# Loading two batches' values with a cast in the DMA, more zero matmuls early on, and later spreads, in a fused attention and feed-forward kernel

## The chip, the cores and the metric

One core of a Trainium2 chip. The metric is the device time of one execution in microseconds (us). Most executions of one kernel lie within about 1% of each other. Each is put down as fast or slow: for a program on one core, slow means over 1.5% above the fastest execution of the same kernel. Verdicts use fast runs alone, with a 95% interval. Profiles are single executions, and so one profile shows one of the states that a kernel can be in. That matters more than usual here.

## The reference, cut to what matters

```python
# q, k, v: (8 batches, 8 heads, 576 tokens, 64)   window 32, dilation 4
mask_plain = (rel >= 0) & (rel < window)                       # heads 0 to 3
mask_dil   = (rel >= 0) & (rel < 4 * window) & (rel % 4 == 0)  # heads 4 to 7
attn = softmax(where(mask, q @ k.T / 8, -1e9)) @ v             # per batch and head
x = attn.transpose(0, 2, 1, 3).reshape(4608, 512)
h = x @ w_in                                                   # 512 -> 2048
out = (h * sigmoid(beta * h)) @ w_out                          # 2048 -> 512
```

The feed-forward part is TensorE's bulk: about 1,000 matmuls of 512 columns. The attention of batch b + 1 is woven into the feed-forward of the tokens of batch b. Only the attention of the first batch has nothing to hide behind.

Of the kernel before, what the change touches and what calls it, by code (L numbers as in the profile page):

```python
# [9 lines left out]
BF16 = mybir.dt.bfloat16  # L10
# [10 lines left out]
).split()  # L21

FIRST = (
    "W10 K2 W2 Q2 W2 K3 S20 S21 Q3 W1 S22 S23 z0 S30 S31 S32 S33 v0 W2 V20 V21 K0 W1 v1 V22 K1 V23 W1 Q0 "
    "V30 W1 V31 W1 X20 S00 V32 S01 V33 X21 S02 v4 S10 X30 S11 V00 S12 X31 V01 H0 v5 X00 V10 H1 X01 V11 X10 X11 "
    "z1 z2"
).split()
SECOND = (
# [16 lines left out]
def kernel(  # L45
# [10 lines left out]
    nc = tc.nc  # L56
    P = 128
    B, H, S, D = q.shape
# [4 lines left out]
    WIN = 32  # L63
    C = 4
# [44 lines left out]
    ident_f = const([NFB, NFB], FP32, "ident_f")  # L109
# [17 lines left out]
    vp = [const([P, 4, NI, DV], BF16, f"vp{i}") for i in range(2)]  # L127
    vd = [const([P, 2, 4, C, DV], BF16, f"vd{i}") for i in range(2)]
    vp_st = [const([P, 4, NI, D], FP32, f"vp_st{i}") for i in range(2)]
    vd_st = const([P, 2, 4, C, D], FP32, "vd_st")  # L130


    k1 = [xT[:, 2 * i:2 * i + 2, 2 * S:2 * S + WIN + S] for i in range(2)]
    q1 = [qq[i][:].rearrange("p a b c d -> p (a b c d)").rearrange(
# [5 lines left out]
    for n, x in ((n, x) for x in (1, 0) for n in "kq"):  # L140
        R, T = (48, 12) if x else (64, 9)
# [13 lines left out]
    def zeros():  # L155
        nc.vector.memset(warm_w[:], 0.0)
        nc.vector.memset(warm[:], 0.0)
        for hf in range(2):
            nc.vector.memset(neg_d[hf][:], 0.0)
        nc.vector.memset(neg_p[:], 0.0)  # L160
        nc.vector.memset(qzd[0][64:128, 0], 0.0)
        nc.vector.memset(qzd[0][0:64, 1], 0.0)
        nc.vector.memset(vp_st[0][0:WIN, 0, 0], 0.0)
        for x in range(4):
            nc.vector.memset(pt[x][:, pt_w[x]:], 0.0)
        for x in range(2, 4):
            nc.vector.memset(pt[x][64:96, 8 * DQ[0]:8 * DQ[0] + 32], 0.0)
        for i in range(2):
            nc.vector.memset(vd[i][:, :, :, :, D:D + 1], 1.0)
            nc.vector.memset(k1[i][:, :, 0:WIN], 0.0)  # L170
            nc.vector.memset(vp[i][:, :, :, D:D + 1], 1.0)
        nc.vector.memset(plain_T["k"][:, 0:WIN // 2], 0.0)
# [7 lines left out]
    def band(flat, w, lo, hi, yes, no):  # L180
        if yes:
            nc.gpsimd.memset(flat, yes)
        if len(flat.shape) == 2:
            flat = flat.unsqueeze(1)
        r = flat.shape[1]
        nc.gpsimd.affine_select(
            out=flat, in_=flat, pattern=[[0, r], [1, w]], base=-lo,
            channel_multiplier=-1, compare_op=ALU.is_ge, fill=no)
        nc.gpsimd.affine_select(
            out=flat, in_=flat, pattern=[[0, r], [-1, w]], base=hi,  # L190
            channel_multiplier=1, compare_op=ALU.is_ge, fill=no)
# [9 lines left out]
    def build_neg_p():  # L201
        band(neg_p[:], QT, -WIN, -1, 0.0, -NEG)
        nc.gpsimd.memset(neg_p[0:WIN, 0], -NEG)
# [31 lines left out]
    def load_w_in(c0, c1):  # L235
        nc.gpsimd.dma_start(
            out=w_in_bf[:, :, c0:c1], in_=moe_w_in[:, c0:c1].rearrange("(c p) d -> p c d", p=P))

    def load_w_out(g):
        nc.gpsimd.dma_start(  # L240
            out=w_out_bf[:, g * 4:(g + 1) * 4, :],
            in_=moe_w_out[g * 4 * P:(g + 1) * 4 * P, :].rearrange("(c p) d -> p c d", p=P))
# [15 lines left out]
    def load_tok(b, n, x, h0=0, nh=4):  # L258
        R, T = (48, 12) if x else (64, 9)
        src = {"q": q, "k": k}[n][b, 4 * x + h0:4 * x + h0 + nh].rearrange("h (a T) d -> a h (T d)", T=T)  # L260
        nc.gpsimd.dma_start(out=tok[n, x][:, h0:h0 + nh], in_=src)  # L261
# [21 lines left out]
    def copy_on(eng):  # L283
        return eng.copy if eng is nc.scalar else eng.tensor_copy
# [20 lines left out]

    def load_vp_1(b, eng, n=0, m=4 * NI, p=0):
        eng.dma_start(
            out=vp_st[b % 2][:].rearrange("p h i d -> p (h i) d")[p:P, n:n + m],
            in_=bass.AP(tensor=v.tensor, offset=v[b, 0].offset + (QT * n - WIN + p) * D,
                        ap=[[D, P - p], [QT * D, m], [1, D]]))  # L310

# [9 lines left out]

    def load_vd(b, eng):
        rows = v[b, 4:8].rearrange("h (t T) d -> t h (T d)", T=C)
        st = vd_st[:].rearrange("p f h T d -> p f h (T d)")
        for hf in range(2):
            eng.dma_start(out=st[0:DK[hf], hf], in_=rows[DO[hf]:DO[hf] + DK[hf]])


    def cast_v(b, n, eng):
        if n == 2 or n > 3:  # L330
            h = slice(0, 4) if n == 2 else slice(2 * n - 8, 2 * n - 6)
            copy_on(eng)(out=vp[b % 2][:, h, :, 0:D], in_=vp_st[b % 2][:, h])
        else:
            f, K = (slice(n, n + 1), DK[n]) if n < 2 else (slice(0, 2), 96)
            copy_on(eng)(  # L335
                out=vd[b % 2][0:K, f].rearrange("p f h T e -> p (f h T) e")[:, :, 0:D],
                in_=vd_st[0:K, f].rearrange("p f h T d -> p (f h T) d"))


    for b in range(2):  # L340
# [144 lines left out]
    def attention_step(b, name):  # L485
        if name[0] == "W":
            for n in range(int(name[1:])):
                nc.tensor.matmul(warm_ps[:], lhsT=warm_w[:, 0:P], rhs=warm_w[:], start=True, stop=True)
        elif name[0] == "H":
            early[0] = -1  # L490
            slot_h(0, int(name[1:]), (2, 3))
        elif name[0] in STEP:
            STEP[name[0]](b, *[int(c) for c in name[1:]])
        else:
            eng = (nc.scalar if name[0] == "v" and (b, name) in ((2, "v2"),) else
                   nc.gpsimd if b == 0 and name in ("v1", "v4", "v5") else nc.vector)
            BRING[name[0]](b, int(name[1:]), eng)


# [90 lines left out]
    def steps(b):  # L590
        return SECOND if b == 1 else THIRD if b == 2 else FOURTH if b == 3 else STEPS

    def extras(b):
        e = {}
        at = lambda name, fn, *a: e.setdefault(steps(b).index(name), []).append(lambda: fn(*a))
        V, A, G = nc.vector, nc.scalar, nc.gpsimd
        SQ = nc.sync
        if b + 1 < B:
            if b > 1:
                if b == 2:  # L600
                    at("S20", gate, raw[2, "q"][0:1, 0:1])
                for kind in "kq":
                    at("S20", cast_qk, b + 1, kind)
                if b == 2:
                    at("S20", cast_v, b, 0, G)
                    at("S20", cast_v, b, 1, G)
                at("X20", load_vd, b + 1, SQ)
                at("X20", load_vp, b + 1, SQ)
            if b == 1:
                at("X20", load_vd, b + 1, SQ)  # L610
                at("X20", load_vp, b + 1, SQ)
                at("V10", spread_dil, b + 1, 0, V)
                at("V11", spread_dil, b + 1, 1, V)
                at("X01", spread_k, b + 1, 0, V)
                at("X10", spread_k, b + 1, 1, V)
            if b > 1:
                for kind in "kq":
                    at("V21", load_dil, b + 1, kind)
                for kind in "kq":
                    at("V30", load_plain, b + 1, kind)  # L620
            if b > 1:
                at("S11", spread_dil, b + 1, 0, V)
                at("V01", spread_dil, b + 1, 1, V)
                at("X00", cast_v, b + 1, 3, G)
                at("X01", cast_v, b + 1, 2, G)
        return e


    SQ, G, A, V = nc.sync, nc.gpsimd, nc.scalar, nc.vector
# [16 lines left out]
    load_tok(0, "q", 0)  # L646
    load_vp_1(0, G, 0, 1, WIN)
    load_vp_1(0, G, 1, 2 * NI - 1)
    load_vp_1(0, G, 2 * NI, 2 * NI)
    for name in FIRST:  # L650
        if name == "v1":
            attention_step(0, "v1")
            build_neg_p()
            for c0, c1 in ((0, 256), (256, 512), (512, 1024)):
                load_w_in(c0, c1)
            continue
        if name == "v5":
            load_w_in(1024, 1536)
            for n in "kq":
                load_tok(1, n, 1)  # L660
            load_w_in(1536, 2048)
            make_identity(nc, ident_f[:])
        if name == "X10":
            build_beta()
        attention_step(0, name)
    load_w_out(0)
    for n in "kq":
        load_tok(1, n, 0)
    load_w_out(1)
    G.memset(vd_st[64:96, 1], 0.0)  # L670
    load_vd(1, G)
    load_w_out(2)
    load_vp_1(1, G)
# [7 lines left out]
    for n in range(2):  # L681
        cast_v(1, n, G)
    zeros_kz()
    for n in (4, 5):
        cast_v(1, n, G)
    build_masks_d()
    build_masks_p()

# [5 lines left out]
    for t in range(NTT):  # L694
        slots = []
        n = len(left)
# [14 lines left out]
        b = t + 1  # L711
        work = list(enumerate(steps(b))) if b < B else []
        e = extras(b) if b < B else {}
# [4 lines left out]
        for n, (fn, *args) in enumerate(slots):  # L718
            fn(*args)
            seen += room[n] if n < len(room) else 0  # L720
            while work and (done * total < whole * seen if t else len(e0) - len(work) < first(n)):
                m, name = work.pop(0)
# [37 lines left out]
```

## The kernel before: the parts that the change and the argument touch

A string gives the order of steps of each batch's attention: S is scores and exponential, V the product with the values, X the transpose into the feed-forward's input, K and Q the transposes of keys and queries, v a cast of values, z a zeroing, W some matmuls on zeros that only keep TensorE's clock up. A **spread** is a copy by VectorE of transposed keys or queries into the layout that the score matmuls read. The digits are the pair of heads (0 and 1 plain, 2 and 3 dilated) and the part.

```python
FIRST = (
    "W10 K2 W2 Q2 W2 K3 S20 S21 Q3 W1 S22 S23 z0 S30 S31 S32 S33 v0 W2 V20 V21 K0 W1 v1 V22 K1 V23 W1 Q0 "
    "V30 W1 V31 W1 X20 S00 V32 S01 V33 X21 S02 v4 S10 X30 S11 V00 S12 X31 V01 H0 v5 X00 V10 H1 X01 V11 X10 X11 "
    "z1 z2").split()
SECOND = (... "S02 V33 S10 X21 S11 V00 X30 S12 V01 X31 V10 X00 V11 X01 X10 X11").split()
THIRD  = ("S20 S21 S22 q0 S23 V20 S30 q1 V21 S31 ...").split()
```

GpSimd's queue issues the loads of the first two batches. Queries, keys and weights are cast to bf16 by the load itself. The values are loaded in float32 and cast afterwards: `vd_st` and `vd` are those of the dilated heads, `vp_st` and `vp` those of the plain heads.

```python
load_tok(0, ...dilated heads...); load_vd(0, G); load_tok(0, "k", 0); load_tok(0, "q", 0)
load_vp_1(0, G, ...)                     # three pieces
for name in FIRST:
    if name == "v1": attention_step(0, "v1"); build_neg_p(); load_w_in(0..1024) ; continue
    if name == "v5": load_w_in(1024, 1536); load_tok(1, ..., 1); load_w_in(1536, 2048); make_identity(...)
    attention_step(0, name)
load_w_out(0); load_tok(1, ..., 0); load_w_out(1); load_vd(1, G); load_w_out(2); load_vp_1(1, G)
for kind in "kq": cast_qk(2, kind)       # third batch's keys and queries: bf16 copy in DRAM, the "scratch"
for kind in "kq": load_dil(2, kind)      # SyncE: DMA transposes of the scratch
for kind in "kq": load_plain(2, kind)
...                                      # SyncE, behind them: third batch's values, float32
```

Two moments come back in all that follows. **K0** is TensorE's first transpose of the first batch's plain-head keys. The **value product** is the first product with the third batch's values, step V20 of THIRD. It needs TensorE to have got there, and it needs that batch's values, loaded behind the transposes of the scratch, cast by GpSimd, and two score tiles masked by GpSimd behind the casts.

The softmax here doesn't subtract the row's maximum and nothing guards it: scores larger than these inputs give would overflow.

## Time and profile before

| | before |
|---|---|
| median of the runs first given | 331.46 us (331.16 to 332.13) |
| the profiled execution | 335.36 us, slow; span 333.7 us, mean granted clock 0.990 |
| TensorE | 95% of the span |
| VectorE, ScalarE, GpSimd | 58%, 59%, 41% |
| two stretches at half clock, 3.4 us each | from 17.1 us and from 64.9 us |
| value product | 73.5 us |

The span is from the first to the last instruction; about 1.7 us of the timed execution lie outside it. The profiled execution was 4 us slower than the median. The prediction below read this profile as if it were an ordinary run.

### The profile page before, as it was taken

To read this page: it belongs to the slowest core of one execution; us is meant where nothing else is said; L and a number is where in the kernel's file an instruction comes from. 1 tells how busy PE (TensorE), PEld (TensorE's weight loads), DVE (VectorE), ACT (ScalarE), POOL (GpSimd) and SP (SyncE) were. 2 spreads that over 40 slices of the span, in tenths; PEclk is the share of its full clock that TensorE was granted. 3 is DMA by queue.
4 is the path that set the end of the run, shared out by engine and by line. 5 is a ranking of instruction groups with operands and counts; after the bars stand their busy time and mean duration, and the time that the engine had idled before them with its cause. 6 is when DMAs were issued, how large, how long until landed. Compare 5 with 4: busy or idle time off the path is not lost.

```text
span 333.7 us, 6338 instructions
## 1 busy us (share of the span) xinstructions
PE 315.5 (95%) x2382; PEld 168.8 (51%) x2426; DVE 192.8 (58%) x431; ACT 195.4 (59%) x378; POOL 137.0 (41%) x179
## 2 busy tenths in 40 slices
PE   8698999698989999999999999999999999999995
PEld 3574466344555555555555555555555544444444
DVE  4568764568655975777377737773766344344400
ACT  3577674366666676666566666666666545355511
POOL 8684359554266347534653365335533000000000
PEclk9979999899999999999999999999999999999999
DMA  6999999999997895999497958791011210011131
GB/s 106 192 187 191 223 238 178 182 192 222 196 141 155 142 191 111 172 191 165 91 171 167 163 102 155 187 152 56 10 31 33 63 32 33 32 33 31 31 95 65
DMA packets 65455, 42.63 MB, mean 128 GB/s; under 512 B 48912, under 2 KB 59824, under 8 KB 65040
## 3 DMA queue, kind: packets, MB, share of 16 engines
q1 hardware_dynamic: 57264, 25.58, 42.1%
q0 software_dynamic: 8160, 16.64, 28.2%
q8 instruction: 19, 0.31, 0.4%
q14 instruction: 12, 0.10, 0.1%
HBM read 39.32 MB, written 16.52 MB: 167 GB/s over the span
## 4 chain that ended last, share of the span: by engine, by line
PE 71%; DMA 15%; POOL 4%; DVE 3%; SPq 2%; issue 2%; ACT 2%; POOLq 0%; ACTq 0%; DVEq 0%
PE h_ps L511 30%; PE o_ps L549 26%; PE at L549 5%; DMA qk<-in_q_dram 5%; DMA xT<-in_k_dram 4%; DMA vp_st<-in_v_dram 3%; PE at L449 3%; DMA vd_st<-in_v_dram 2%; PE at L466 2%; PE at L416 2%; PE at L423 2%; DVE g L521 1%; POOL xT L261 1%; SPq L279 1%; PE at L568 1%
## 5 line engine op out<-in xcount | busy, mean ns | idle before, releaser
L521 DVE SCALAR_TENSOR_TENSOR g<-tnh,h_ps 128x512 bf16<-128x512 bf16 x130 | 88.9, 684 | 91.4 <-ACT tnh L518 90.7
L511 PE MATMUL h_ps<-xT,w_in_bf 128*128 128x512 bf16 x503 | 129.8, 380 | 3.0 <-DVE g L521 1.6
L518 ACT ACTIVATE tnh<-h_ps,beta_half 128x512 bf16<-128x512 f32 x130 | 89.3, 687 | 56.4 <-PE h_ps L511 53.8
L549 PE MATMUL o_ps<-w_out_bf,g 128*128 128x512 bf16 x443 | 113.6, 379 | 1.2
L511 PEld LDWEIGHTS <-w_in_bf 128*128 128x128 bf16 x576 | 52.0, 98 | 51.6 <-issue 4.0
L549 PEld LDWEIGHTS <-g 128*128 128x128 bf16 x560 | 50.6, 98 | 47.8 <-issue 0.6
L429 ACT ACTIVATE pt<-at 128x384 bf16<-128x384 f32 (+2 forms) x107 | 46.1, 438 | 15.2 <-PE at L416 7.4
L431 POOL TENSOR_TENSOR pt<-pt,mask_d 96x384 bf16<-96x384 bf16 (+1 forms) x48 | 36.9, 780 | 40.5 <-ACT pt L429 39.9
L456 DVE TENSOR_TENSOR xs<-at,rcp 48x256 bf16<-48x256 f32 (+2 forms) x91 | 42.2, 463 | 8.2 <-PE at L466 4.0
L431 POOL TENSOR_TENSOR pt<-pt,mask_PP 128x384 bf16<-128x384 bf16 x24 | 22.7, 945 | 37.2 <-ACT pt L429 37.1
L449 PEld LDWEIGHTS <-pt 128*128 128x128 bf16 (+2 forms) x448 | 24.5, 98 | 16.8 <-issue 1.3
L557 ACT ACTIVATE osb<-o_ps 128x512 f32<-128x512 f32 x28 | 16.7, 597 | 19.0 <-PE o_ps L549 18.7
L466 PE MATMUL at<-ident_b,xs 96*128 96x96 bf16 (+1 forms) x224 | 18.5, 201 | 3.4 <-DVE xs L456 2.8
L466 PEld LDWEIGHTS <-xs 96*128 96x128 bf16 (+1 forms) x224 | 13.7, 97 | 14.4 <-DVE xs L456 4.1
L452 DVE RECIPROCAL rcp<-at 48x4 f32<-48x4 f32 (+2 forms) x91 | 16.1, 176 | 8.3 <-PE at L449 7.5
L549 PE MATMUL at<-w_out_bf,g 128*128 128x512 bf16 x79 | 19.3, 379 | 0.1
L423 PEld LDWEIGHTS <-kdT 128*96 128x96 bf16 (+1 forms) x128 | 14.3, 120 | 9.9 <-issue 0.3
L449 PE MATMUL at<-vd,pt 96*128 96x65 bf16 (+1 forms) x244 | 17.6, 194 | 1.6 <-DVE vd L335 0.7
L335 POOL CAST vd<-vd_st 96x2048 bf16<-96x2048 f32 (+2 forms) x10 | 14.6, 1460 | 10.6 <-DMA vd_st<-in_v_dram 7.3
L431 POOL TENSOR_TENSOR pt<-pt,mask_FP 128x384 bf16<-128x384 bf16 x12 | 10.9, 910 | 18.5 <-ACT pt L429 18.5
L423 PE MATMUL at<-qzd,kdT 128*80 128x96 bf16 (+1 forms) x122 | 17.1, 226 | 0.1
L480 ACT COPY xT<-at 128x384 bf16<-128x384 bf16 (+1 forms) x32 | 12.7, 396 | 4.9 <-PE at L466 4.9
(115 smaller groups left out, 255.2 us busy)
## 6 DMA issues: line engine op xcount, KB each, us to landing
vp_st<-in_v_dram SPq DMA_DIRECT2D x12, 384.0 KB, 8.8
qk<-in_k_dram POOLq DMA_DIRECT2D x6, 576.0 KB, 6.1
qk<-in_q_dram POOLq DMA_DIRECT2D x6, 576.0 KB, 9.9
vd_st<-in_v_dram SPq DMA_DIRECT2D x6, 384.0 KB, 5.4
w_out_bf<-in_moe_w_out_dram POOLq DMA_DIRECT2D x4, 512.0 KB, 17.0
vd_st<-in_v_dram SPq DMA_DIRECT2D x6, 320.0 KB, 6.5
out_dram<-osb SPq DMA_DIRECT2D x7, 256.0 KB, 3.6
out_dram<-osb SPq DMA_DIRECT2D x8, 224.0 KB, 2.4
```

The source lines that it names most:

```text
L423: nc.tensor.matmul(sc[0:K, a, 0:2 * n], lhsT=kd[b][:, rp, h4, DO[hf]:DO[hf] + K], rhs=qzd[b % 2][:, :, rp, h4, hf * DQ[0]:hf * DQ[0] + n], ...
L429: nc.scalar.activation(out=w, in_=sc[0:K, :, 0:2 * n], func=ACT.Exp, scale=SCALE)
L431: nc.gpsimd.tensor_tensor(out=w, in0=w, in1=mask[0:K], op=ALU.mult)
L449: nc.tensor.matmul(pv[:, a, h2, :], lhsT=pt[x][0:K, c:c + P], rhs=rhs, start=True, stop=True)
L452: nc.vector.reciprocal(out=rcp[0:n, 0:m], in_=pv[0:n, :, :, D])
L456: nc.vector.tensor_tensor(out=xs_t[b, x, jx][:, a0:a0 + m], in0=pv[0:n, :, :, 0:D], in1=rcp[0:n, 0:m].unsqueeze(3).to_broadcast([n, m, 2, ...
L466: nc.tensor.transpose(xp[:, a * n:(a + 1) * n], xs[:, a].rearrange("p h d -> p (h d)"), ident_b[0:n, 0:n])
L511: nc.tensor.matmul(hps, lhsT=w_in_bf[:, kt, fb * P:(fb + 1) * P], rhs=xT[:, kt, t * NTOK:(t + 1) * NTOK], start=(kt == 2), stop=(kt == 1))
L518: nc.scalar.activation(out=tnh[:], in_=hps, func=ACT.Tanh, scale=beta_half[:, fb:fb + 1])
L521: nc.vector.scalar_tensor_tensor(out=g[:], in0=tnh[:], scalar=1.0, in1=hps, op0=ALU.add, op1=ALU.mult)
L549: nc.tensor.matmul(ops[:], lhsT=g_t[t, fb][:, tb * P:(tb + 1) * P], rhs=w_out_bf[:, fb, :], start=(fb == 0), stop=(fb == NFB - 1))
L557: nc.scalar.mul(out=osb[:], in_=ops[:], mul=0.5)
```

## The change

Its intent: take the casts of the first two batches' values off GpSimd and let the loads do them; with GpSimd free, issue the weight loads at once; keep TensorE's clock up in the first attention with 14 more zero matmuls; and let VectorE finish the second batch before it waits for the third batch's transposes.

```diff
-    "... Q3 W1 S22 S23 z0 S30 S31 S32 S33 v0 W2 V20 V21 K0 W1 v1 V22 K1 V23 W1 Q0 "
-    "V30 W1 V31 W1 X20 S00 V32 S01 V33 X21 S02 v4 S10 ... H0 v5 X00 ..."
+    "... Q3 W2 S22 S23 S30 W1 S31 S32 W1 S33 v0 z0 W3 V20 V21 v1 W3 K0 W2 V22 K1 W3 V23 Q0 W2 "
+    "V30 W2 V31 W2 X20 S00 V32 S01 V33 X21 S02 S10 ... H0 X00 ..."
 ...
+    vd_sb = <4 KB a partition of vp_st[1], seen as bf16>
 ...
-            out=vp_st[b % 2][:].rearrange("p h i d -> p (h i) d")[p:P, n:n + m],
+            out=vp[b % 2][:].rearrange("p h i d -> p (h i) d")[p:P, n:n + m, 0:D],
 ...
-        st = vd_st[:].rearrange("p f h T d -> p f h (T d)")
+        st = vd_sb if b < 2 else vd_st[:].rearrange("p f h T d -> p f h (T d)")
 ...
-                at("V10", spread_dil, b + 1, 0, V)
-                at("V11", spread_dil, b + 1, 1, V)
-                at("X01", spread_k, b + 1, 0, V)
-                at("X10", spread_k, b + 1, 1, V)
+                at("X10", spread_dil, b + 1, 0, V)
+                at("X10", spread_dil, b + 1, 1, V)
+                at("X11", spread_k, b + 1, 0, V)
+                at("X11", spread_k, b + 1, 1, V)
 ...
+    build_neg_p()                                  # ahead of the last piece of load_vp_1(0)
+    for c0, c1 in ((0, 256), (256, 512), (512, 1024), (1024, 1536)):
+        load_w_in(c0, c1)                          # all ahead of the first attention
```

Step v1 moves from GpSimd to VectorE, and v4 and v5 and the second batch's casts of plain values go.

More of the change, by code (lines that the diff above doesn't have):

```diff
@@ L23 @@
 FIRST = (
-    "W10 K2 W2 Q2 W2 K3 S20 S21 Q3 W1 S22 S23 z0 S30 S31 S32 S33 v0 W2 V20 V21 K0 W1 v1 V22 K1 V23 W1 Q0 "
-    "V30 W1 V31 W1 X20 S00 V32 S01 V33 X21 S02 v4 S10 X30 S11 V00 S12 X31 V01 H0 v5 X00 V10 H1 X01 V11 X10 X11 "
+    "W10 K2 W2 Q2 W2 K3 S20 S21 Q3 W2 S22 S23 S30 W1 S31 S32 W1 S33 v0 z0 W3 V20 V21 v1 W3 K0 W2 V22 K1 W3 V23 Q0 W2 "
+    "V30 W2 V31 W2 X20 S00 V32 S01 V33 X21 S02 S10 X30 S11 V00 S12 X31 V01 H0 X00 V10 H1 X01 V11 X10 X11 "
     "z1 z2"
@@ L130 @@
     vd_st = const([P, 2, 4, C, D], FP32, "vd_st")
+    vd_sb = vp_st[1][:].rearrange("p h i d -> p (h i d)").bitcast(BF16)[:, 0:8 * C * D].rearrange(
+        "p (f h e) -> p f h e", f=2, h=4)
     k1 = [xT[:, 2 * i:2 * i + 2, 2 * S:2 * S + WIN + S] for i in range(2)]
@@ L162, in zeros @@
         nc.vector.memset(qzd[0][0:64, 1], 0.0)
-        nc.vector.memset(vp_st[0][0:WIN, 0, 0], 0.0)
+        nc.vector.memset(vp[0][0:WIN, 0, 0, 0:D], 0.0)
         for x in range(4):
@@ L329, in cast_v @@
     def cast_v(b, n, eng):
-        if n == 2 or n > 3:
-            h = slice(0, 4) if n == 2 else slice(2 * n - 8, 2 * n - 6)
-            copy_on(eng)(out=vp[b % 2][:, h, :, 0:D], in_=vp_st[b % 2][:, h])
+        if n == 2:
+            copy_on(eng)(out=vp[b % 2][:, :, :, 0:D], in_=vp_st[b % 2][:])
         else:
             f, K = (slice(n, n + 1), DK[n]) if n < 2 else (slice(0, 2), 96)
+            src = vd_sb.rearrange("p f h (T d) -> p f h T d", T=C) if b < 2 else vd_st[:]
             copy_on(eng)(
                 out=vd[b % 2][0:K, f].rearrange("p f h T e -> p (f h T) e")[:, :, 0:D],
-                in_=vd_st[0:K, f].rearrange("p f h T d -> p (f h T) d"))
+                in_=src[0:K, f].rearrange("p f h T d -> p (f h T) d"))
     for b in range(2):
@@ L495, in attention_step @@
             eng = (nc.scalar if name[0] == "v" and (b, name) in ((2, "v2"),) else
-                   nc.gpsimd if b == 0 and name in ("v1", "v4", "v5") else nc.vector)
+                   nc.vector)
             BRING[name[0]](b, int(name[1:]), eng)
@@ L648 @@
     load_vp_1(0, G, 1, 2 * NI - 1)
+    build_neg_p()
     load_vp_1(0, G, 2 * NI, 2 * NI)
+    for c0, c1 in ((0, 256), (256, 512), (512, 1024), (1024, 1536)):
+        load_w_in(c0, c1)
+    make_identity(nc, ident_f[:])
     for name in FIRST:
-        if name == "v1":
-            attention_step(0, "v1")
-            build_neg_p()
-            for c0, c1 in ((0, 256), (256, 512), (512, 1024)):
-                load_w_in(c0, c1)
-            continue
-        if name == "v5":
-            load_w_in(1024, 1536)
-            for n in "kq":
-                load_tok(1, n, 1)
-            load_w_in(1536, 2048)
-            make_identity(nc, ident_f[:])
         if name == "X10":
@@ L665 @@
         attention_step(0, name)
+    for n in "kq":
+        load_tok(1, n, 1)
+    load_w_in(1536, 2048)
     load_w_out(0)
@@ L669 @@
     load_w_out(1)
-    G.memset(vd_st[64:96, 1], 0.0)
     load_vd(1, G)
@@ L683 @@
     zeros_kz()
-    for n in (4, 5):
-        cast_v(1, n, G)
+    G.memset(vd_st[64:96, 1], 0.0)
     build_masks_d()
```

## The prediction

> **What bounds the kernel now.** I read the page's first two parts first, then the chain of waits between 20 and 80 us, then the waits of TensorE and GpSimd, and last a table of stretches for the stall before 75 us.
>
> ```profile
> PE 315.5 (95%) x2382; PEld 168.8 (51%) x2426; DVE 192.8 (58%) x431; ACT 195.4 (59%) x378; POOL 137.0 (41%) x179
> ...
> PEclk9979999899999999999999999999999999999999
> DMA  6999999999997895999497958791011210011131
> ```
>
> TensorE is busy 95% of the span, and from about 95 us on it hardly ever waits. A change confined to the first 75 us, as this one is, can therefore win only by letting that dense stretch start sooner. The clock row dips twice, near 17 and near 65 us. The DMA row is full until about 100 us.
>
> ```profile
> 23.59 14.90 DMA xT<-in_k_dram
> 38.49 0.28 issue
> 38.78 17.37 DMA qk<-in_q_dram
> 56.14 0.02 issue
> 56.16 2.79 SPq L270
> ...
> 60.39 2.54 SPq L279
> ...
> 63.66 7.76 DMA vd_st<-in_v_dram
> ...
> 71.54 1.04 POOL vd L335
> 72.58 1.76 POOL pt L431 x2
> 74.34 0.05 issue
> 74.38 0.20 PE at L449
> ```
>
> This is the chain of waits (start, length, what). The second batch's tokens land at 38.5, the third batch's queries and keys reach their scratch in DRAM at 56.1, SyncE then issues four transposes and behind them the third batch's values. These land at 71.4, GpSimd casts them (1.04 us), masks two score tiles (1.76 us), and only then can TensorE do its first product with the third batch's values, at 74.38. From 23.6 to 74.4 the chain has no TensorE work in it.
>
> ```profile
> PE at L466 <- DVE xs L456: 2.8, 2, 1.7
> PE at L449 <- POOL pt L431: 0.6, 1, 0.6
> ```
>
> These are TensorE's waits from 62 to 75 us. It stands 2.8 us for VectorE at the end of the second batch, yet at 74.4 it still waits 0.6 us for GpSimd. So it came to the end of that chain only about 0.6 us too early, although it had stood still and then run slowly:
>
> ```profile
> 61.50:64.90 3.40, 1.21 (x8) 0.35 (x5) 1.79 (x6) 1.22 (x4) 0.50 (x2) 1.00 0.76 145
> 64.90:68.30 3.40, 2.82 (x10) 1.17 (x11) 2.14 (x4) 0.99 (x2) 1.42 (x3) 0.50 1.06 203
> 68.30:71.70 3.40, 3.40 (x20) 1.80 (x19) 1.65 (x3) 2.37 (x5) 1.19 (x2) 1.00 1.48 190
> ```
>
> The columns are the stretch, its length, busy time and count of PE, PEld, DVE, ACT and POOL, granted clock, DMA share, GB/s. TensorE works 1.21 us of 3.40, and the next 3.4 us run at half clock.
>
> **What the Trainium skill says.** "TensorE: Matmul & The Clock Gate", Part 1, says that a window of about 3.4 us with too little TensorE activity halves the clock and a busy one restores it, and that the windows run free of the kernel. The trace agrees: two half-clock stretches of 3.4 us, each after a stretch with TensorE idle for more than a third. "DMA: Bandwidth & Descriptors", section "SWDGE vs HWDGE vs iDMA", says that a DMA that casts has to be issued from GpSimd; here all casting loads are, and so only the first two batches' values, which GpSimd already loads, can take part. The same page, "Why small descriptors are slow", says a fixed overhead per packet makes short ones slow. The packet records agree: casting loads took 60 ns for a packet of 512 bytes landed and about 100 ns for 1024, not half.
>
> **The change part by part.**
> (1) Values cast by the DMA. The order of the loads in GpSimd's queue stays what it was, and that queue is never empty from 3 to 54 us (packet records, 1.2 to 1.25 packet times per engine on average from 17 us), so issuing the weight loads 3 to 4 us sooner buys at most 0.2 us. What matters is how long the values themselves take. They are 704 and 768 KB a batch (sizes in the DMA issues), twice.
> Dilated heads: now 176 packets of 4096 bytes a batch at about 280 ns over 16 engines, 3.1 us of packet time. Cast, 704 rows land as 512 bytes; at the 60 ns of w_in's packets that is 2.6 us. Saved 0.45, divided by 1.25 for the overlap, twice: about 0.7 us earlier.
> Plain heads: now about 190 packets at 350 ns (first batch) and 254 ns (second), mean 300, 3.6 us. Cast, 3072 rows land as 128 bytes with gaps between them, so I expect single packets. The line through 60 and 100 ns gives about 28 ns for 128 bytes, 5.4 us; the plain 256-byte packets of the transposes, which took 18 to 23 ns, give 3.8 us. That is 0.2 to 1.8 us more a batch, by 1.25, twice: 0.3 to 2.9 us later. But the uncast loads moved only 191 GB/s (13.5 to 18 us) where casting ones read near 390 GB/s (18 to 19.5 us, 196 GB/s landed), so they can also gain up to a microsecond each. I take 0.4 later.
> Sum: the end of the scratch load about 0.3 us earlier, within plus or minus 1.5. Everything behind it up to 74.38 moves by the same amount, because each link (transposes 56.2 to 62.9, third batch's values 63.1 to 71.4, cast, masks) is untouched.
> (2) Engine work removed: two GpSimd casts of 0.82 us in the first batch and two in the second, and a cast of 1.03 us goes from GpSimd to VectorE (there 0.62 us before, less from bf16). The second product with these values is at 22.5 us, 3.4 us after its cast: none of it is on TensorE's path.
> (3) Zero matmuls: 14 more of 512 columns, 14 x 0.216 = 3.0 us of TensorE, put where it is idle (2.6 us from 10 to 20 us) and where the clock is halved (17.1 to 20.5). Keeping the clock up is worth up to 1.7 us, half of 3.4. The first attention ends perhaps 1 us sooner, or no sooner.
> (4) Spreads moved: the first half-spread waits 2.27 us for its transpose (landed 62.8) ahead of VectorE's work for V10 and V11. Moved behind it, X10 can start at 62.4 instead of 64.1, and TensorE loses neither the 2.8 us nor the half clock: the next matmuls of L511 start at about 63.8 instead of 67.4, and the cold part gives 1 us more. Some 4 to 5 us.
> So parts 3 and 4 bring TensorE to the third batch's first value product at about 69 to 70. Its inputs are there at about 74.0. It then waits about 4 us instead of 0.6. This is the main step of the prediction: **the stall is moved by some ten microseconds, not removed.**
> What stays: 0.3 us from the DMA. VectorE, which at 75.16 was behind (a 1.64 us query spread and a gate product ended at 75.2, the product it should have worked on at 74.6), will have caught up in the stall: 0.7 us, since the chain after 76 us runs through VectorE. Against it, a 4 us stall should halve the clock again, and about half a window, 0.9 us, falls behind 74; TensorE waits 1.4 us for VectorE between 78 and 86 anyway, so I charge 0.5. Sum: -0.3 - 0.7 + 0.5 = -0.5 us, 331.46 to 330.9.
>
> **The rivals.**
> A: the casting loads run at the full read rate. The values, about 12 us of the queue by the rates above, would need 3.0 MB at some 400 GB/s, 7.5 us; the third batch would come 4 to 5 us sooner, the stall would be short and the clock would hold: about 326. For it speaks that the weights do reach that rate; against it, that their rows are 1 to 2 KB at the source and the plain heads' only 256 bytes.
> B: 128-byte writes are much slower than I think, 40 ns or more each: 192 x 20 ns more a batch and engine, 3.1 us by 1.25, twice. The third batch's values land 6 us later, TensorE stands for 10 us: about 337. The packet times of the 256-byte transposes speak against it.
> C: TensorE's own time is what counts, and the end moves by all of the 2.8 us, the cold stretches and the first attention: 326 to 327. The wait of 0.6 us at 74.38 behind an untouched chain speaks against it.
> D: the new stall falls badly in the clock's windows and two half-clock windows follow: 332.5.
>
> **Range and chances.** The DMA term gives plus or minus 1.5 us, the clock term plus or minus 1, the run's own spread 0.5. The range is 328.3 to 333.3 around 330.9. Faster by 2% needs 324.8, more than rivals A or C give alone: 0.06. Slower by 2% needs 338.1, worse than rival B: 0.04. Within 2%: 0.90.
>
> **What would show it.** Right: the half-clock stretch at 65 us is gone, TensorE's 2.8 us wait for VectorE is gone, and in their place it waits 3 us or more for GpSimd's masked scores at the third batch's first value product, which stays within 1.5 us of 74.4; from there on the two traces run side by side. The first two batches' plain values show as short packets of 20 to 28 ns. Wrong: the scratch load lands more than 2 us away from 56.1, in either direction, or the product starts at 70 us, which would mean that the third batch's values did not hang on the chain that I read; or the first attention ends later than 27 us by so much that TensorE is late at the value product.

## The result, and the profile after

| | runs | median, us | range, us |
|---|---|---|---|
| before, same chip | 4 | 331.31 | 330.48 to 332.13 |
| changed | 4 | 328.91 | 328.73 to 329.23 |

The ratio is 0.9929, with an interval of 0.9902 to 0.9955. A ratio is the mean time of one kernel's fast runs over that of the other's of the same rounds, so it is not quite the ratio of the medians. The gain is 2.4 us, 0.7%: within 2%, inside the stated range, but about five times the predicted 0.5 us.

The page of the changed kernel, its lines on busy time, clock and DMA, and its chain of waits by engine:

```profile
PE 314.7 (96%) x2395; PEld 168.7 (52%) x2440; DVE 192.4 (59%) x432; ACT 195.6 (60%) x378; POOL 133.1 (41%) x174
...
PEclk9999999999999999999999999999999999999999
DMA  6999999999989798896869778872101210011131
...
PE 90%; DVE 5%; ACT 3%; issue 2%; DVEq 0%; ACTq 0%
```

Both dips of the clock row are gone, and so is every DMA in the chain. The same stretches as in the prediction, in this kernel:

```profile
61.50:64.90 3.40, 3.40 (x19) 1.53 (x17) 2.98 (x6) 2.43 (x5) 2.56 (x5) 1.00 1.22 222
64.90:68.30 3.40, 3.35 (x25) 1.91 (x25) 2.82 (x4) 2.77 (x8) 2.88 (x4) 1.00 1.27 220
68.30:71.70 3.40, 3.40 (x23) 1.85 (x24) 2.61 (x6) 2.64 (x5) 2.02 (x3) 1.00 0.89 188
```

TensorE is busy throughout at full clock. The answer on TensorE's waits between 62 and 75 us is empty. So the stall at the end of the second batch went, and it did not come back at the value product, which starts at 68.0 us. That is not what the main step of the prediction said.

The spans differ by 333.7 - 327.5 = 6.2 us, while the timed medians differ by 2.4. Most of the difference between these two profiles is one between a slow and a fast run, and may not be explained by the change. So the first experiment was the kernel before, once more.

### The profile page after: what moved, and what is told of

It reads as the page before. It is cut to its first block, busy times and chain, and to the rows that moved or that the text cites. A ratio compares the mean times of both kernels' runs of the same rounds, so it can differ in the third digit from the quotient of the medians.

```text
span 327.5 us, 6356 instructions
## 1 busy us (share of the span) xinstructions
PE 314.7 (96%) x2395; PEld 168.7 (52%) x2440; DVE 192.4 (59%) x432; ACT 195.6 (60%) x378; POOL 133.1 (41%) x174
## 4 chain that ended last, share of the span: by engine, by line
PE 90%; DVE 5%; ACT 3%; issue 2%; DVEq 0%; ACTq 0%
PE h_ps L514 32%; PE o_ps L552 28%; PE at L552 5%; PE at L452 4%; PE at L514 4%; PE o_ps L491 3%; PE at L469 3%; PE at L426 2%; PE at L419 2%; DVE g L524 2%; DVE xs L459 1%; ACT tnh L521 1%; PE at L571 1%; PE at L407 1%; PE at L355 1%
## 5 line engine op out<-in xcount | busy, mean ns | idle before, releaser
L452 PEld LDWEIGHTS <-pt 128*128 128x128 bf16 (+2 forms) x448 | 24.5, 97 | 15.8 <-issue 1.0
L469 PEld LDWEIGHTS <-xs 96*128 96x128 bf16 (+1 forms) x224 | 13.5, 96 | 11.5 <-issue 2.6
L426 PEld LDWEIGHTS <-kdT 128*96 128x96 bf16 (+1 forms) x128 | 14.3, 120 | 9.8
L452 PE MATMUL at<-vd,pt 96*128 96x65 bf16 (+1 forms) x244 | 17.4, 193 | 0.3 <-ACT qq L391 0.3
L514 PE MATMUL at<-xT,w_in_bf 128*128 128x512 bf16 x54 | 13.6, 379 | 0.2
```

The costliest lines, as they stand in the source:

```text
L426: nc.tensor.matmul(sc[0:K, a, 0:2 * n], lhsT=kd[b][:, rp, h4, DO[hf]:DO[hf] + K], rhs=qzd[b % 2][:, :, rp, h4, hf * DQ[0]:hf * DQ[0] + n], ...
L452: nc.tensor.matmul(pv[:, a, h2, :], lhsT=pt[x][0:K, c:c + P], rhs=rhs, start=True, stop=True)
L469: nc.tensor.transpose(xp[:, a * n:(a + 1) * n], xs[:, a].rearrange("p h d -> p (h d)"), ident_b[0:n, 0:n])
L514: nc.tensor.matmul(hps, lhsT=w_in_bf[:, kt, fb * P:(fb + 1) * P], rhs=xT[:, kt, t * NTOK:(t + 1) * NTOK], start=(kt == 2), stop=(kt == 1))
```

## The experiments

Twelve runs, in three calls of four, each call on a chip of its own beside 11 runs of the kernel before. All gave correct results, and all profiles were of fast runs. Two theories at first. Theory 1: the chain of loads sets when the third batch's values are ready, and it became shorter. Theory 2: TensorE's stall and half clock were what counted.

**r1: the kernel before, unchanged.** No edit.

> The kernel before once more, unchanged, to get a profile of a fast run: the profiled run of before was slow (335.4 us against 331.3). If the slow state is only the two half-clock stretches, a fast profile lacks one or both and the third batch's first value product still starts near 74 us, since the load chain is the same. If the loads themselves were slower in that run, the scratch load lands before 56 us by 2 to 4 us and the product starts at 70 to 72 us. Time: ratio 1.000 within 0.3%.

332.34 us median (331.19 to 333.46), ratio 0.9971 (0.9931 to 1.0011). Its profile is of a run of 331.28 us. Three lines of its page and chain (in the chain, start and length in us):

```profile
PE 86%; DVE 5%; ACT 3%; issue 2%; DMA 2%; POOL 1%; ACTq 0%; DVEq 0%; POOLq 0%
...
6.79 6.80 DMA xT<-in_k_dram
16.65 1.57 PE at L364 x36
```

In a fast run of the same kernel the chain does not come through the third batch's loads. It waits for the first batch's plain-head keys, which land at 13.6 us, goes to K0 (L364), and from there runs mostly through TensorE to the end. The value product, with GpSimd's work ahead of it (start, length, engine, line, instruction):

```profile
66.90 1.04 POOL L335 CAST vd<-vd_st 80x1024 bf16<-80x1024 f32 x1 [0.27 <-DMA vd_st<-in_v_dram]
...
68.39 3.10 POOL L431 TENSOR_TENSOR pt<-pt,mask_d 96x384 bf16<-96x384 bf16 x4 [0.45 <-ACT pt L429]
...
70.07 0.45 PE L449 MATMUL at<-vd,pt 96*128 96x65 bf16 x4
```

The mask waited for ScalarE's exponential, not for the cast, and TensorE waited for nothing. But there was next to no room: two masks of some 0.9 us from 68.39 end at about 70.2, in the middle of the product. A half clock shows too, at another place than in the slow run:

```profile
10.77:14.17 3.40, 1.70 (x34) 1.08 (x32) 2.35 (x7) 1.02 (x4) 1.85 (x4) 1.00 1.25 198
14.17:17.58 3.41, 3.05 (x57) 2.47 (x56) 1.18 (x4) 1.28 (x2) 3.30 (x5) 0.50 1.11 213
17.58:20.99 3.41, 3.41 (x40) 2.44 (x37) 1.90 (x6) 2.55 (x5) 3.33 (x7) 0.50 1.35 201
```

So the second expectation held: the loads were later in the slow run (scratch landed 56.1 us there, 54.2 here). What follows: the chain that the prediction was built on belongs to a slow run, or rather to the upper end of one spread: at 335.4 us it was only 1.5% above the fastest, and one of the 33 runs counted as fast beside these experiments took 335.5. In the fast profile the two arrivals at the value product meet within about 0.2 us, so by this profile alone moving only one of them should win little. r2 will not fit that.

**r2: the casting loads alone.**

```diff
+ casting loads of vp and vd for batches 0 and 1, GpSimd's casts of vp out
  (zero matmuls, spreads, v1 on GpSimd, place of the w_in loads: as before)
```

> Only the casting loads of the first two batches' values; zero matmuls, spreads and the place of the weight loads as before. Theory 1 (the load chain sets when the third batch's values are ready, and it became shorter): the scratch load lands 2 to 4 us sooner and the time falls by most of the 2.4 us, to 329 to 329.8. Theory 2 (TensorE's stall and half clock at the end of the second batch were what counted, the loads were hidden): within 0.5 us of before, 331.

329.84 us (328.39 to 330.66), ratio 0.9892 (0.9854 to 0.9930). As good as the whole change. The scratch landed at 52.8 us, 1.5 us sooner than in r1. Theory 1 by its time; but its profile says that there is more to it. K0 starts at 12.80 instead of 13.63 us, and the profiled span is only 0.7 us below r1's, the product waiting 0.4 us for the masks. But that profile is of the slowest of these six runs (330.66 us), and r1's of nearly the fastest of its own. Between the medians, 332.61 us of the kernel before and 329.84, lie 2.8 us, and between the fastest runs, 331.21 and 328.39, as many. So these two profiles show only a part of the gain. The weight loads are issued as late here as in the kernel before: the early issue is not needed for the gain.

**r3: the zero matmuls alone.** The edit is the W and z0 of FIRST as in the diff, with v4 and v5 kept.

> Only the zero matmuls, doubled and placed as in the changed kernel. Theory 1: no effect, within 0.5 us of before, because TensorE then only waits longer at 74 us; the half-clock stretch at 17 us is gone in the profile. Theory 2: 0.5 to 1.5 us faster, since TensorE's own time is what counts.

334.34 us (332.77 to 335.57), ratio 1.0037 (0.9997 to 1.0078): no gain, rather a loss. The half clock in the first attention is gone and TensorE reaches the end of the second batch earlier, only to wait for VectorE, which waits for the transposes. A half-clock stretch follows there:

```profile
PE at L466 <- DVE xs L456: 2.2, 2, 1.1
```

```profile
60.60:64.00 3.40, 1.20 (x11) 0.59 (x11) 3.13 (x8) 0.82 (x3) 1.37 (x3) 1.00 1.02 205
64.00:67.40 3.40, 3.40 (x10) 1.20 (x9) 1.11 (x3) 1.28 (x2) 0.33 (x2) 0.50 1.27 157
```

**r4: the spreads alone.** The edit is the four lines of the diff.

> Only the third batch's spreads at the end of the second. Theory 1: the 2.8 us wait for VectorE goes and comes back as a wait of 3 us or more for GpSimd's masked scores at the third batch's first value product; time within 0.5 us of before. Theory 2: 1.5 to 2.5 us faster.

333.20 us (331.59 to 334.39), ratio 0.9994 (0.9954 to 1.0034). The wait for VectorE went, and 0.6 us of wait for GpSimd's masks came: in kind as theory 1 had it, but not the 3 us, since a fast run has no 2.8 us stall to begin with.

After these four neither theory stood as written. I went on with theory M, that the value product starts at the later of two arrivals, against theory L, that the loads alone set it, and put the parts together in pairs.

**r5: the changed kernel again.** No edit.

> The changed kernel again, on the chip of the next three, so that they can be compared with it. Theory M (the third batch's first value product starts at the later of two arrivals: TensorE's, and the values', cast and masked): both about 68 us, ratio near 0.990. Theory L (the loads alone set it): the same here.

329.28 us (329.02 to 330.19), ratio 0.9911 (0.9891 to 0.9932).

**r6: the changed kernel with the old zero matmuls.**

```diff
- Q3 W2 S22 S23 S30 W1 S31 S32 W1 S33 v0 z0 W3 V20 V21 v1 W3 K0 W2 V22 K1 W3 V23 Q0 W2 V30 W2 V31 W2
+ Q3 W1 S22 S23 S30 S31 S32 S33 v0 z0 W2 V20 V21 v1 K0 W1 V22 K1 V23 W1 Q0 V30 W1 V31 W1
```

> The changed kernel with the old number of zero matmuls. Theory M: TensorE is at half clock in the first attention again, as in the kernel before (two windows from 14 us), and comes 0.5 to 1.5 us later to the value product, 68.5 to 69.5 us, without waiting there; time 0.5 to 1.5 us over the changed kernel. Theory L: the values are as early as in the changed kernel, so time as the changed kernel within 0.3 us.

329.58 us (328.30 to 331.40), ratio 0.9918 (0.9887 to 0.9949). The median is the same; the six runs fall into 328.3 to 328.9 and 330.2 to 331.4. The profiled one, of 328.44 us, had no half clock in the first attention. There TensorE was at the product by 66.9 us and then waited 0.3 us for the masks. What I expected of theory M, half clock and a later arrival, did not show in the profile; the runs above 330 us may be of that kind. A timed run does not record where its clock dipped, but it does record its mean: 0.995, 0.990 and 0.989 in the three runs above 330 us, 1.000, 1.000 and 0.993 in the three below. In all ten runs of the changed kernel it is 0.997 to 1.000.

**r7: the changed kernel with the spreads at their old place.** The edit is the four lines of the diff, undone.

> The changed kernel with the spreads at their old place. Theory M: the transposes now land 3 to 5 us sooner, but TensorE comes sooner too, so a part of its wait for VectorE at the end of the second batch is back: 0.5 to 2 us[...]; time 0.3 to 2 us over the changed kernel. If the transposes land before VectorE gets to the spreads: no difference. Theory L: no difference.

330.00 us (329.37 to 330.06), ratio 0.9925 (0.9906 to 0.9945): 0.7 us over r5 by the medians, 0.7 by the profiled spans, and 0.7 us of wait for VectorE in the trace. Theory M; theory L, which saw no difference, falls, though single runs of the two overlap.

**r8: zero matmuls and spreads of the changed kernel, values loaded as before.** The edits of r3 and r4 together.

> The kernel before with the zero matmuls and the spreads of the changed kernel, but the values loaded as before. Theory M: TensorE is at the value product at 68 to 68.5 us and waits 1.5 to 2.5 us there for GpSimd's masks; time as before, 331 (ratio 0.998 to 1.002). Theory L: the same time. If TensorE's side were all that counts: as the changed kernel.

333.80 us (332.85 to 337.29), ratio 1.0055 (1.0014 to 1.0097). This run is what the prediction expected of the whole change, but without the casts:

```profile
69.34 1.04 POOL L335 CAST vd<-vd_st 80x1024 bf16<-80x1024 f32 x1 [0.45 <-PE at L511]
70.34 2.79 POOL L431 TENSOR_TENSOR pt<-pt,mask_d 96x384 bf16<-96x384 bf16 x4
...
71.31 0.35 PE L449 MATMUL at<-vd,pt 96*128 96x65 bf16 x3 [2.06 <-POOL pt L431]
```

```profile
67.90:71.30 3.40, 1.35 (x10) 0.52 (x8) 1.94 (x3) 1.62 (x5) 2.95 (x4) 1.00 1.40 225
71.30:74.70 3.40, 2.87 (x12) 1.35 (x13) 0.60 (x2) 0.54 (x1) 1.83 (x3) 0.50 0.94 201
```

TensorE comes early and stands, in all 2.6 us, for masks that queue behind the casts of late values; then its clock is halved. The stall is moved and not removed, and it costs: the kernel is slower than before. In the changed kernel, on the same chip, the same instructions (its L452 is L449 here) read:

```profile
64.44 1.12 POOL L338 CAST vd<-vd_st 80x1024 bf16<-80x1024 f32 x1 [0.20 <-DMA vd_st<-in_v_dram]
...
66.39 3.09 POOL L434 TENSOR_TENSOR pt<-pt,mask_d 96x384 bf16<-96x384 bf16 x4 [0.83 <-ACT pt L432]
...
68.07 0.44 PE L452 MATMUL at<-vd,pt 96*128 96x65 bf16 x4
```

The cast starts 4.9 us sooner, and the mask waits for the score tile and no longer for the cast. What makes the loads sooner, the casts or GpSimd's earlier issue, and which casts, was the last question.

**r9: early issue without casting loads.**

```diff
- casting loads of vp and vd
+ float32 loads as before; VectorE casts the first batch's values at v0, v1, v4 and v5
  (everything else as in the changed kernel)
```

> The changed kernel with the values loaded uncast again, but GpSimd still free of the first batch's casts (VectorE does them), so that the weight loads are still issued early. Theory R (it is the time of the values in the load queue that counts): first batch's value loads end near 18 us, scratch load starts near 47 us as without the casts, TensorE waits 1.5 to 2.5 us for GpSimd's masks at the third batch's value product; ratio to before 1.000 to 1.006. Theory I (it is the early issue): scratch load starts near 44.5 us, no wait, ratio 0.991 to 0.994.

330.95 us (330.50 to 334.18), ratio 0.9963 (0.9922 to 1.0004). The loads fit theory R: first scratch packet at 46.8 us, against 47.7 in r8 and 43.5 in r5. But TensorE did not wait at the product. It came there later, since the first attention took 0.8 us longer than in r5 once VectorE had those casts to do. So this run does not separate the early issue cleanly. In the load queue it is worth no more than the scatter of single runs: the six with float32 values have their first scratch packet at 45.8 to 48.4 us. Yet the ratio is 0.9% below r8's, with intervals apart. In the profiles TensorE is 1.1 us later at the first tanh than in r8, the cast of the third batch's values 2.1 us sooner, and so there is no stall. How much of that is the early issue stays open.

**r10: only the dilated heads' values cast by their loads.** As r9, but `vd` loaded with a cast, into half of `vd_st`.

> The changed kernel with only the dilated heads' values cast by their loads. If the saving is in the 4096-byte packets of these (as the prediction had it, 0.45 us of packet time a batch): the scratch load starts about 2 us sooner than uncast, near 45.5 us, ratio 0.992 to 0.997. If it is the plain heads: near 47 us, ratio 1.000 or above.

330.34 us (329.78 to 330.60), ratio 0.9929 (0.9899 to 0.9959). First scratch packet at 44.0 us: nearly all of the saving.

**r11: only the plain heads' values cast by their loads.** `vd` loaded in float32, the rest as changed.

> The changed kernel with only the plain heads' values cast by their loads. The prediction had 128-byte packets cost 0.4 us in sum: then the scratch load starts near 47 us and the ratio is 1.000 or above. If they save as much as the dilated heads: near 45.5 us, ratio 0.992 to 0.997.

331.20 us (329.57 to 332.77), ratio 0.9957 (0.9917 to 0.9997). First scratch packet at 46.0 us, 1.0 us sooner than uncast on average, not later as the prediction had it, but within the scatter of the uncast runs. The six runs fall into 329.6 to 330.3 and 332.1 to 332.8; the profiled one (332.77 us) is the slowest, waits 1.9 us for the masks and has its half clock from 71.7 us, like r8.

**r12: casting loads and early issue, without the other two parts.** The edits of r6 and r7 together.

> Casting loads and early issue, with the old zero matmuls and the spreads at their old place: a candidate for a kernel as fast as the changed one with two of its three parts left out. If the casts are all of it: ratio 0.989 to 0.992. If the other parts protect the clock in some runs: the same median within 0.3% but a spread of 2 us or more between runs, against about 1 us for the changed kernel.

329.54 us (328.70 to 330.93), ratio 0.9919 (0.9880 to 0.9957): 0.8 of the 0.9% that the whole change had in r5, with a spread of 2.2 us against 1.2. Four of its six runs have a mean clock of 0.989 to 0.993, among them the three above 330 us. No run beat the changed kernel clearly; r2, r6 and r12 are as fast within their intervals.

**The timed runs alone.** With all values cast by their loads the ratio is 0.989 to 0.993 (the first result, r2, r5, r6, r7, r12), with float32 loads 0.996 to 1.006 (r1, r3, r4, r8, r9), whatever the other parts are. r1 is the unchanged kernel, so 0.3% of this is noise. With one of the two kinds cast it is 0.993 (r10, dilated) and 0.996 (r11, plain). So the casting loads make the gain. Zero matmuls and spreads move the ratio by 0.14% at most in the three runs on one chip that differ in them alone (r5, r6, r7), and win nothing without the casting loads (r3, r4, r8). By which path the loads do it is read from single profiles, and is less sure.

**All profiles in one table.** Each time is read from the timeline: K0, from there to the first tanh of the feed-forward, from there to the value product, and from there to the end of the span, in us. "Scratch" is the start of the second DMA transpose, which waits for the scratch to land.

| run | K0 | to tanh | to product | to end | span | scratch |
|---|---|---|---|---|---|---|
| before, slow | 14.74 | 13.15 | 45.64 | 260.2 | 333.7 | 56.2 |
| r1 before | 13.63 | 14.46 | 41.98 | 259.5 | 329.6 | 54.2 |
| r3 zeros | 13.14 | 13.12 | 45.32 | 259.5 | 331.1 | 54.2 |
| r4 spreads | 14.01 | 14.43 | 41.35 | 260.1 | 329.9 | 54.9 |
| r8 zeros, spreads | 14.34 | 13.12 | 43.85 | 261.4 | 332.7 | 55.7 |
| r9 + early issue | 14.29 | 14.23 | 41.36 | 259.5 | 329.4 | 54.8 |
| r11 plain cast | 13.51 | 13.43 | 42.82 | 261.3 | 331.1 | 53.7 |
| r10 dilated cast | 13.65 | 14.24 | 41.51 | 259.4 | 328.8 | 51.6 |
| r2 casts alone | 12.80 | 14.27 | 41.97 | 259.9 | 328.9 | 52.8 |
| r12 casts, issue | 12.44 | 13.06 | 41.97 | 259.5 | 327.0 | 51.4 |
| r7 no spreads | 13.43 | 13.41 | 41.97 | 259.5 | 328.3 | 52.7 |
| r6 no zeros | 12.12 | 13.39 | 41.36 | 259.8 | 326.7 | 52.1 |
| r5 changed | 13.29 | 13.42 | 41.36 | 259.5 | 327.6 | 51.6 |
| changed, first | 13.17 | 13.47 | 41.36 | 259.5 | 327.5 | 52.0 |

Read down the columns. After the product every run takes 259.4 to 260.2 us, or 261.3 to 261.4 where a half-clock window falls behind it. Between tanh and product it is 41.4 to 41.5 us with late spreads and 41.97 with early ones, unless TensorE waits (r3 for VectorE, r8 and r11 for GpSimd, the slow run for VectorE and then, at half clock, for GpSimd). From K0 to tanh it is 13.1 to 13.5 us at full clock, 14.3 to 14.5 with 6.8 us of half clock there (r1, r2, r4), and 14.2 where VectorE casts the plain values. In the slow run, with 3.4 us of half clock there, it is 13.15: that half clock cost nothing that shows.

K0 is 13.95 us on average of the seven runs with float32 loads of the dilated values, and 12.99 in the seven with casting ones: that load is ahead of the first batch's plain-head tokens in the queue. But single runs overlap (13.1 to 14.7 and 12.1 to 13.7), and something else sets K0 in the changed kernel. First r1, then r5:

```profile
13.63 0.65 PE L364 MATMUL h_ps<-ident_b,xT 64*64 64x64 bf16 x18 [0.99 <-DMA xT<-in_k_dram]
```

```profile
12.55 0.81 PE L491 MATMUL o_ps<-warm_w 128*128 128x512 bf16 x3
13.29 0.65 PE L367 MATMUL h_ps<-ident_b,xT 64*64 64x64 bf16 x18
```

With the old zero matmuls TensorE waits for the keys (in all but r6), and casting loads bring K0 from 13.6 to 14.7 us (slow run, r1, r4) to 12.1 to 12.8 (r2, r6, r12). In r5 it comes straight from the added zero matmuls. So these have a price: r6 and r12, at full clock without them, reach tanh at 25.5 us, r5 at 26.7. What they seem to buy is the even clock and the narrow spread of the changed kernel; the medians of r5 and r6 are within 0.3 us. The casting loads help the clock too: with the old zero matmuls, 7 of 18 timed runs with casting loads (r2, r6, r12) have a mean clock of 0.998 or more, and 1 of 45 with float32 loads (the kernel before, r1, r4).

So r1 to r5 is 0.34 us at K0, 1.04 for the clock, 0.62 for the spreads: 2.0 us, all of 329.6 - 327.6. All three lie on TensorE's own path, and the 0.34 is within the scatter of K0. The third batch's earlier values add nothing to this sum, but r8 shows that without them the rest is lost. It is the sum of two single profiles, r1's near the fastest of its kernel and r5's the median of its own, and not of the medians.

## Why the prediction was right or wrong

**The range was right, the size was too small, and the step named as the main one failed.** "The stall is moved by some ten microseconds, not removed" describes r8 and not the changed kernel. The step was that TensorE comes to the value product at 69 to 70 us, finds its inputs ready only at 74.0 and waits 4 us. Measured: the last cast of these inputs starts at 64.4 us (r5), TensorE is there at 68.0 to 68.1 and waits for nothing. Two of the prediction's own signs of being wrong came true: the second transpose, which waits for the scratch, started at 52.0 us, 4.1 before 56.1, and the product came even before 70. That the result lies in the range owes nothing to the stall that was forecast; the range was wide enough for another mechanism.

**The bound (wrong for fast runs).** The chain from 23.6 to 74.4 us without TensorE was there, in a slow run. In the fast run r1 the chain passes through TensorE from 13.6 us on, and the product starts at 70.1 us. The prediction set the profile's slow state aside and took the median of fast runs as its starting point. The half clock at 65 us and the 2.8 us wait, from which part (4) worked out 4 to 5 us, are not in r1 either: the wait is 0.7 us there, and moving the spreads is worth 0.6 us (r7 against r5).

**Term (1), the loads (mechanism right, size wrong).** "About 0.3 us earlier, within plus or minus 1.5" was 2.9 us: the scratch column averages 55.0 us over the six runs with all values in float32 and 52.1 over the six with all of them cast. The packet durations were read nearly right: 61 ns for 512 bytes, 33 ns for 128 bytes (predicted 60 and 28; the line through 60 and 100 ns gives 30). The fault was to add up durations and divide by one overlap for all kinds. How many packets run side by side differed between kinds: the DMA share below is 1.04, 1.21, 1.06 and 2.00. The bytes that landed in a stretch are the better measure. Two stretches of the first batch's dilated values, float32 in r8 and cast in r5 (last columns clock, DMA share, GB/s landed):

```profile
7.00:10.00 3.00, 3.00 (x49) 2.03 (x47) 1.72 (x4) 2.33 (x7) 3.00 (x5) 1.00 1.04 241
```

```profile
7.00:9.00 2.00, 1.36 (x20) 0.96 (x20) 0.91 (x2) 1.02 (x4) 2.00 (x4) 1.00 1.21 170
```

With a cast 170 GB/s landed are 340 GB/s read, against 241 read uncast. For 704 KB (0.72 MB) that is 2.1 us instead of 3.0, 0.9 us less, near the 1.0 us between the averages of K0. And the plain values, landing in 128-byte rows:

```profile
13.50:18.00 4.50, 3.66 (x86) 2.85 (x86) 2.01 (x8) 1.28 (x2) 4.29 (x8) 1.00 1.06 191
```

```profile
12.00:16.00 4.00, 4.00 (x62) 2.30 (x60) 2.77 (x8) 1.50 (x4) 3.58 (x7) 1.00 2.00 155
```

191 GB/s read became 310, with a DMA share of 2.00 in place of 1.06: the divisor of 1.25 was far off just here. (Both stretches hold some packets of other loads. Where nearly all are values, 14.0 to 17.0 us in r8 and 12.5 to 14.5 in r5, it is 199 against 300.) The 191 stood in the prediction, as a doubt, and should have been the estimate. The shares were wrong too: r10 and r11 put about 3 us of the scratch's advance on the dilated values and 1 us on the plain ones, where the prediction had 0.7 and minus 0.4. The two do not add up to 2.9 exactly, since loads of single runs differ by 1 to 2 us.

**Part (2), engine work: right.** No cast taken off GpSimd was on TensorE's path. What the prediction missed is that in the kernel before the load of the dilated values was on it, by way of K0 (r1 waits 0.99 us there).

**Part (3), zero matmuls: right in size, wrong in its value.** From K0 to tanh 1.0 us less where they prevent 6.8 us of half clock (r1 against r5). In the profile of r6, where none occurred without them, there was nothing to gain, and they cost 1.2 us at K0. Alone (r3) the time did not fall, because of what comes after.

**The 0.7 us for a VectorE that catches up, and the 0.5 us for the clock: did not apply,** as there was no stall. From the product on the traces run side by side, as the last part of the prediction said: 259.5 us in both r1 and r5. The half clock of a moved stall is real, at 1.9 us in r8 (261.4 against 259.5).

**The rivals.** A had its first half come true: the third batch's values came sooner, by 2.5 us from r1 to r5 and 4.9 from r8, and the stall did not appear. Its 326 us rested on the slow run's chain. C, TensorE's own time, is the arithmetic of the gain between r1 and r5, but only with A's loads; r8 shows C alone at 1.0055. The 328.9 us lie between the prediction and both.

**What stays open.** Why the fast runs of the kernel before scatter from 330.5 to 335.5 us and those of the changed one, ten runs, only from 328.7 to 330.2. The slow profile suggests that late loads and a half clock at 65 us belong to the upper end, and the changed kernel has room against both; but timed runs leave no trace, so this is argued and not shown. Their mean clocks do not settle it: in the runs of the kernel before it is 0.987 to 0.995 below 332 us and 0.984 to 0.994 above 334. Open too are the share of the early issue (r9) and the path by which r2 gains the whole.

## What to carry to other kernels

Before you build on a chain of waits, compare the profiled execution's time with the timed median; if it lies well above, take another profile, because its chain may be that of another state. Where two arrivals meet at one instruction, work out both before and after the change: shortening one alone can even cost time, as r8 shows with a stall and a half clock. Compare medians before you sum up two profiles: each of the two may be the best or the worst run of its kernel. Size a load by the bytes that it moved in its own stretch, not by the durations of its packets.

## What the Trainium skill lacked or had wrong

- "DMA: Bandwidth & Descriptors" says that a cast needs a DMA issued from GpSimd, but has no figure for its speed. Here the casting load of 704 KB of values read about 340 GB/s where the plain float32 load read 241, and one with 256-byte source rows and 128-byte destination rows read about 300 against 199.
- The same page, "Why small descriptors are slow", gives a fixed overhead for each packet; taken alone, that would make a load with 128-byte destination rows a bad trade. The packets were short indeed (33 ns on average for 128 bytes, 61 ns for 512), but about two per engine were in flight at once (DMA share 2.00 against 1.06), and the load became faster.
- "TensorE: Matmul & The Clock Gate", Part 1, gives the half clock after an idle window, and no share of busy time below which a window counts as idle. Windows of 3.4 us in which TensorE was busy for 1.20 (r3), 1.35 (r8) and even 1.70 us (r1) were followed by a half clock as well.
- "GPSIMD Engine Reference" gives rates for two-input arithmetic; for a copy it gives none by the type of the source. A copy of 96 x 1024 elements there gained nothing from a bf16 source: 1.03 us from float32 and about 1.0 from bf16 (two in 2.01 us, r5), while VectorE went from 0.62 us (r1) to 0.42 (r5).
